# A decode block on one core: the engines' programs written into the main program instead of a block

## The chip, the core and the metric

The kernel runs on one core of a Trainium2 chip. Its time is the device time of one execution in microseconds (us); the median of several runs is given. A profile shows one execution, with times counted from the first instruction of the program to the last (the span). The core has five engines with programs of their own: TensorE (PE; its weight loads are PEld), VectorE (DVE), ScalarE (ACT), GpSimd (POOL) and SyncE (SP), which issues DMAs only. They meet through semaphores.

## The reference

One decode step for a batch of 8: a conditioning vector gives six modulation rows, then a grouped-query attention over a cache of 8192 keys, then a gated feed-forward part. Cut to what is computed:

```python
mod = (silu(c) @ w_mod).reshape(8, 6, 1, 1024)          # sa, ca, ga, sb, cb, gb
h = layernorm(x) * (1 + ca) + sa
q = (h @ wq)                                            # 32 heads of 128, 4 key/value heads
p = softmax(q @ k_cache^T * 128**-0.5)                  # 8 x 32 x 8192
x = x + ga * ((p @ v_cache) @ wo)
h = layernorm(x) * (1 + cb) + sb
g = h @ W_gate; g = g * (g > 0)
x = x + gb * ((g * (h @ W_up)) @ W_down)                # 8 x 1 x 1024, bf16
```

All inputs are bf16. The caches are 67 MB each; with the weights 185.6 MB are read from HBM.

## The kernel before, in words

Everything that is read passes through one ring buffer in SBUF, five slots of 4 MB. SyncE issues all of these loads (line 747), one after the other in an order written out by hand: the query weights, the modulation weights, then 16 pairs of a key block and a value block (two key/value heads of one batch row, 4 MB each), with the output weights between, then the gate, up and down weights. A load that reuses a slot first waits for the last TensorE instruction that read the slot. The small inputs c and x are loaded by ScalarE (line 87).

GpSimd first fills constants. VectorE and ScalarE prepare the conditioning vector; TensorE multiplies it by the modulation weights, then the normalised x by the query weights. The attention is a loop over n, 0 to 17, software-pipelined by hand: in step n TensorE transposes the key block of n (line 426), VectorE and ScalarE copy the transposed keys out of PSUM, TensorE makes the scores (line 422); for n-1 the softmax, the transposition of the weights and the product with the value block follow; for n-2 the sums and the division. Then come the output projection, the second normalisation, gate and up, and the down projection, whose last loads are cut ever smaller (3584 KB to 256 KB). The last two VectorE operations give outR, which goes out in four DMAs, two from SyncE and two from ScalarE (line 87), all counted on one semaphore, osem, 16 each.

The code doesn't call the engines directly. A small graph class collects operations in five lists, one an engine, with what each reads and writes; it thins the dependences out, numbers the semaphores' values, and `emit` writes one list to its engine, operation by operation, with the waits ahead of each (line 117). On TensorE, VectorE and ScalarE the attention's steps 0 to 15 are emitted as a hardware loop of eight turns of two steps (line 158), with waits against a value computed from the turn's number (line 161).

The lists are handed to the engines at the end of the kernel's function. There a block is opened, and each engine's list is emitted in a body of that block; SyncE's body ends with a wait for the four DMAs of the output:

```python
            def body(_, name=name, e=e):
                g.emit(name, e, sems)
                if name == "sp":
                    e.wait_ge(osem, 64)
            starter(body)
```

A body is a stretch of program for one engine. The engine reaches it by a jump from the main program (line 761 is its place in the source) and leaves it by a jump to the block's end. At the block's end, which is written when the context closes (line 269 in the profile), each engine drains, all report to GpSimd by a semaphore event, and GpSimd lets all of them go by another: a closing round. On SyncE the wait for osem is held by the jump that leaves the body. The main program itself begins with four constants on GpSimd and a round of the same kind, the opening round, which is written when the program object is made (line 775).

Of the kernel before, what the change touches and what calls it, by code (L numbers as in the profile page):

```python
# [234 lines left out]
def bass_adaLN_cond__gqa_block_cached__glu_gated_reglu__decode_kernel(  # L235
# [14 lines left out]
    B, _, D = A_x.shape  # L250
    _, G, Sk, Dh = A_k_cache.shape
# [14 lines left out]
    g = _Graph()  # L266
    f32, bf16 = dt.float32, dt.bfloat16

    with ExitStack() as es:
        E = es.enter_context  # L270
# [58 lines left out]
        sems = {e: E(nc.semaphore("m_" + e)) for e in g.prog}  # L329
        csem = E(nc.semaphore("d_c"))  # L330
        xsem = E(nc.semaphore("d_x"))
        osem = E(nc.semaphore("d_o"))
# [412 lines left out]
        for i, (key, at, cols, src, shape, slot) in enumerate(stream):  # L745
# [4 lines left out]
        g.prog["sp"] = head + g.prog["sp"]  # L750
        g.number()

        block_ = E(nc.Block())
        engs = {"sp": (nc.sync, block_.sync), "act": (nc.scalar, block_.scalar), "pool": (nc.gpsimd, block_.gpsimd),
                "dve": (nc.vector, block_.vector), "pe": (nc.tensor, block_.tensor)}
        for name, (e, starter) in engs.items():
            def body(_, name=name, e=e):
                g.emit(name, e, sems)
                if name == "sp":
                    e.wait_ge(osem, 64)  # L760
            starter(body)


# [26 lines left out]
```

## Time and profile before

| what | value |
|---|---|
| median of 3 runs | 438.68 us (438.67 to 438.71) |
| the profiled execution | 438.55 us |
| its span, first to last instruction | 436.6 us |
| mean granted TensorE clock | 0.945 |
| DMA queue of SyncE | 185.61 MB, 98.7% of 16 engines' time |
| busy: PE, ACT, DVE, POOL | 306.9, 208.6, 180.0, 12.7 us |

The execution is 1.95 us longer than the span; what lies in that difference is not in the trace. Rows of the trace name an engine, a line of the source, an operation and the buffers. A q behind an engine's name (SPq) marks work of its sequencer: waiting, jumping, issuing DMAs. It isn't counted as busy. DRAIN is an instruction that lets the engine finish what it has begun, EVENT_SEMAPHORE one that waits for a semaphore or changes it, COMPARE_BRANCH a jump.

### The profile page before, as it was taken

How to read it: one execution, taken by the hardware profiler on the slowest of the kernel's cores; microseconds unless marked ns; L12 is line 12 of the kernel's file. 1: busy time of each engine (PE TensorE's matmuls, PEld its weight loads, DVE VectorE, ACT ScalarE, POOL GpSimd, SP SyncE). 2: the span in 40 equal slices, each digit the busy share in tenths (PEclk: the TensorE clock that was granted, in tenths of full speed). 3: DMA queues.
4: the chain of work that ended last, by engine and by line, in shares of the span. 5: the costliest groups of instructions: out<-in, count | busy, mean ns of one | idle time of the engine just before them, and what ended most of it. 6: DMA issues, size and time to landing. Idle time of an engine off the chain costs nothing.

```text
span 436.6 us, 10734 instructions
## 1 busy us (share of the span) xinstructions
PE 306.9 (70%) x4575; PEld 199.4 (46%) x4575; DVE 180.0 (41%) x384; ACT 208.6 (48%) x246; POOL 12.7 (3%) x52
## 2 busy tenths in 40 slices
PE   0104276889889888787888888778888878755353
PEld 0101024656556555555555556555555555432321
DVE  3600027365463644536264553536354453331111
ACT  2200004676767747675664757576575747400000
POOL 6000000000000000000000000000000000000000
PEclk9999579999999999999999999999999999885778
DMA  8999999999999999999999999999999999999995
GB/s 342 438 446 437 429 431 434 432 428 437 432 441 432 432 432 432 432 435 435 432 432 432 432 432 432 432 432 432 432 432 432 432 432 432 422 435 439 427 422 236
DMA packets 7003, 185.81 MB, mean 426 GB/s; under 512 B 800, under 2 KB 832, under 8 KB 1104
## 3 DMA queue, kind: packets, MB, share of 16 engines
q1 hardware_dynamic: 6928, 185.61, 98.7%
q8 instruction: 9, 0.15, 0.1%
q10 hardware_dynamic: 64, 0.04, 0.0%
q14 instruction: 2, 0.02, 0.0%
HBM read 185.63 MB, written 0.02 MB: 425 GB/s over the span
## 4 chain that ended last, share of the span: by engine, by line
DMA 54%; PE 23%; issue 8%; DVE 8%; ACT 6%; SPq 1%; DVEq 0%; ACTq 0%
DMA ring<-in_A_k_cache_dram 29%; PE PS L426 12%; DMA ring<-in_w_mod_dram 11%; PE PS L422 11%; DMA ring<-in_B_W_down_dram 7%; DMA ring<-in_B_W_up_dram 6%; ACT P L433 3%; DVE KT L430 2%; ACT KT L433 2%; DVE tm L430 1%; DVE ov L430 1%; DVE nm L430 1%; SPq L747 1%; DVE nb L430 0%; DVE rl L430 0%
## 5 line engine op out<-in xcount | busy, mean ns | idle before, releaser
L433 ACT ACTIVATE KT<-PS 128x1024 bf16<-128x1024 bf16 (+1 forms) x130 | 132.1, 1017 | 163.8 <-PE PS L426 137.4
L426 PE MATMUL PS<-identb,ring 128*128 128x128 bf16 x2048 | 152.8, 220 | 19.3 <-DMA ring<-in_A_k_cache_dram 17.6
L430 DVE COPY KT<-PS 128x1024 bf16<-128x1024 bf16 (+1 forms) x129 | 88.9, 689 | 162.5 <-PE PS L426 126.3
L426 PEld LDWEIGHTS PS<-identb,ring 128*128 128x128 bf16 x2048 | 117.0, 98 | 58.5 <-issue 37.3
L422 PE MATMUL PS<-KT,Z 128*32 128x512 bf16 x516 | 51.9, 390 | 0.1
L422 PE MATMUL PS<-ring,pt 128*32 128x256 bf16 x1088 | 49.8, 274 | 0.6 <-DVE pt L430 0.6
L433 ACT ACTIVATE P<-PS,nb 64x1024 bf16<-64x1024 f32 x34 | 37.7, 1109 | 6.2 <-DVE nb L430 4.2
L426 PE MATMUL PS<-identb,P 128*128 128x128 bf16 x272 | 21.0, 221 | 20.2 <-ACT P L433 14.5
L422 PEld LDWEIGHTS PS<-ring,pt 128*32 128x32 bf16 x1088 | 24.5, 95 | 12.8 <-issue 0.8
L422 PE MATMUL PS<-ring,siluT 128*24 128x512 bf16 x96 | 9.8, 584 | 27.5 <-DMA ring<-in_w_mod_dram 27.5
L426 PEld LDWEIGHTS PS<-identb,P 128*128 128x128 bf16 x272 | 15.3, 98 | 26.5 <-DVE KT L430 17.2
L433 ACT ACTIVATE pt<-PS 64x512 bf16<-64x512 bf16 x34 | 20.1, 592 | 13.5 <-PE PS L426 13.2
L430 DVE COPY pt<-PS 64x512 bf16<-64x512 bf16 x34 | 14.4, 422 | 17.7 <-PE PS L426 17.2
L430 DVE TENSOR_REDUCE mp<-PS 128x1 f32<-128x1024 f32 x17 | 20.6, 1214 | 0.0
L422 PEld LDWEIGHTS PS<-KT,Z 128*32 128x32 bf16 x516 | 13.3, 93 | 13.8 <-ACT KT L433 0.5
L422 PE MATMUL PS<-ring,h2T 128*8 128x512 bf16 (+1 forms) x128 | 10.4, 490 | 11.6 <-DMA ring<-in_B_W_up_dram 9.7
L422 PEld LDWEIGHTS PS<-ring,siluT 128*24 128x24 bf16 x96 | 3.1, 125 | 33.5 <-DMA ring<-in_w_mod_dram 28.3
L433 ACT ACT_TABLE_LOAD x11 | 14.1, 1283 | 8.3 <-DMA KT<-in_A_x_dram 8.1
L426 PE MATMUL PS<-identb,KT 128*128 128x128 bf16 (+1 forms) x19 | 1.7, 218 | 18.4 <-DVE KT L430 18.4
L637 POOL CAST ot<-og 128x16 bf16<-128x16 f32 x16 | 4.1, 256 | 288.2 <-DVE og L430 288.2
L422 PE MATMUL PS<-od,selo 128*128 128x128 f32 x36 | 8.8, 326 | 5.1 <-DVE od L430 5.1
L422 PEld LDWEIGHTS PS<-ring,h2T 128*8 128x8 bf16 x128 | 3.5, 108 | 17.8 <-DMA ring<-in_B_W_up_dram 11.0
(99 smaller groups left out, 161.4 us busy)
## 6 DMA issues: line engine op xcount, KB each, us to landing
ring<-in_A_k_cache_dram SPq DMA_DIRECT2D x16, 4096.0 KB, 21.6
ring<-in_A_v_cache_dram SPq DMA_DIRECT2D x16, 4096.0 KB, 30.5
ring<-in_w_mod_dram SPq DMA_DIRECT2D x2, 6144.0 KB, 42.4
ring<-in_A_wq_dram SPq DMA_DIRECT2D x2, 4096.0 KB, 16.8
ring<-in_A_wo_dram SPq DMA_DIRECT2D x2, 4096.0 KB, 28.1
ring<-in_B_W_gate_dram SPq DMA_DIRECT2D x2, 3584.0 KB, 24.8
ring<-in_B_W_up_dram SPq DMA_DIRECT2D x2, 3584.0 KB, 31.0
ring<-in_B_W_down_dram SPq DMA_DIRECT2D x1, 3584.0 KB, 36.1
```

The source lines that it names most:

```text
L422: return pe(lambda e: e.matmul(out_, lhsT, rhs, start=start, stop=stop, skip_group_check=True), reads, writes, block, deps)
L426: return pe(lambda e: e.matmul(out_, in_, ident, start=True, stop=True, is_transpose=True), reads, writes, block)
L430: return g.op("dve", lambda e: getattr(e, name)(*args, **kw), reads, writes)
L433: return g.op("act", lambda e: e.activation(*args, **kw), reads, writes)
L637: pool(lambda e: e.tensor_copy(dst, og[:, n % 2]), reads=[("og", n % 2)], writes=[("ot", n // B)])
L747: o.fn = (lambda e, key=key, src=src, o=o: e.dma_start(place[key], src).then_inc(o.sem, 16))
```

## The change

The block is gone. `emit` is called for the five engines one after the other, in the order SyncE, ScalarE, GpSimd, VectorE, TensorE, and writes their instructions into the main program, behind the opening round. The wait for the output is written last, on SyncE.

```diff
         g.prog["sp"] = head + g.prog["sp"]
         g.number()
 
-        block_ = E(nc.Block())
-        engs = {"sp": (nc.sync, block_.sync), "act": (nc.scalar, block_.scalar), "pool": (nc.gpsimd, block_.gpsimd),
-                "dve": (nc.vector, block_.vector), "pe": (nc.tensor, block_.tensor)}
-        for name, (e, starter) in engs.items():
-            def body(_, name=name, e=e):
-                g.emit(name, e, sems)
-                if name == "sp":
-                    e.wait_ge(osem, 64)
-            starter(body)
+        for name, e in (("sp", nc.sync), ("act", nc.scalar), ("pool", nc.gpsimd), ("dve", nc.vector), ("pe", nc.tensor)):
+            g.emit(name, e, sems)
+        nc.sync.wait_ge(osem, 64)
```

On each engine the operations and their waits stay in the same order. What differs is at the ends: the jump into the body and the jump out of it go, on SyncE the wait that the latter held becomes an instruction of its own, and the block's end goes, that is a drain on each engine, the event by which it reports or is let go, and GpSimd's two events. The opening round stays. The hardware loops stay as they are.

## The prediction

> **What bounds the kernel now.** I read the page first, for the span and the load of each engine.
>
> ```profile
> span 436.6 us, 10734 instructions
> PE 306.9 (70%) x4575; PEld 199.4 (46%) x4575; DVE 180.0 (41%) x384; ACT 208.6 (48%) x246; POOL 12.7 (3%) x52
> DMA  8999999999999999999999999999999999999995
> q1 hardware_dynamic: 6928, 185.61, 98.7%
> q8 instruction: 9, 0.15, 0.1%
> DMA 54%; PE 23%; issue 8%; DVE 8%; ACT 6%; SPq 1%; DVEq 0%; ACTq 0%
> ```
>
> No compute engine is busy for more than 70% of the span, while the one queue that carries the weights and the caches fills 98.7% of sixteen engines' time. The digits of the DMA row are nines from the second slice to the last but one. The kernel is bound by one stream of loads that SyncE issues, and the chain of waits is mostly transfers (54%). So an edit counts only if it moves the start of that stream, stretches it, or lies behind its end. The change touches no operation, load, buffer or semaphore inside the work; it touches the two places where the five programs are joined to the main program. I therefore read the timeline at both ends of the span, then the rows that carry the lines of the frame: L775 (opening round), L761 (jump into the block), L269 (block's end).
>
> The start, from the timeline:
>
> ```profile
> 0.73 0.21 POOL L444 MEMSET identb<- 128x128 bf16 x1 [0.29 <-POOLq L775]
> 0.74 0.89 SPq L747 DMA_DIRECT2D ring<-in_A_wq_dram  x2
> 0.74 0.59 ACTq L87 DMA_DIRECT2D KT<-in_c_dram  x1
> ```
>
> The end, from the timeline of the last 4 us, and SyncE's own waits there:
>
> ```profile
> 432.99 0.09 PEld L422 LDWEIGHTS PS<-ring,hmT 128*8 128x8 bf16 x4 [0.52 <-DMA ring<-in_B_W_down_dram]
> 433.00 0.39 PE L422 MATMUL PS<-ring,hmT 128*8 128x256 bf16 x4 [0.23 <-DMA ring<-in_B_W_down_dram]
> 433.89 0.42 DVE L430 TENSOR_TENSOR outR<-ov,x1R 128x256 bf16<-128x256 f32 x1
> 434.34 0.71 SPq L87 DMA_DIRECT2D out_dram<-outR  x2
> SPq L269 <- DMA out_dram<-outR: 1.1, 1, 1.1
> SPq L269 <- PEq L269: 0.2, 1, 0.2
> ```
>
> The last weights land, four matmuls and two vector operations follow, the output goes out from 434.34 for 0.71 us (to 435.05), SyncE then waits 1.1 us for the output to land (436.2), and only after that does the closing round run, with a second wait of 0.2 us in SyncE. The instructions of that round carry the line of the context that closes, L269:
>
> ```profile
> L269 POOLq EVENT_SEMAPHORE  x2: 17/17/17, 436.4 to 436.5; - x2
> L269 POOLq DRAIN  x1: 341/341/341, 384.5 to 384.5; - x1
> L269 PEldq DRAIN  x1: 442/442/442, 433.0 to 433.0; - x1
> L269 DVEq DRAIN  x1: 464/464/464, 433.9 to 433.9; - x1
> L269 ACTq DRAIN  x1: 239/239/239, 435.0 to 435.0; - x1
> L269 SPq COMPARE_BRANCH  x1: 33/33/33, 436.2 to 436.2; - x1
> L269 SPq DRAIN  x1: 7/7/7, 436.4 to 436.4; - x1
> L269 SPq EVENT_SEMAPHORE  x1: 17/17/17, 436.5 to 436.5; - x1
> L269 PEldq EVENT_SEMAPHORE  x1: 51/51/51, 436.5 to 436.5; - x1
> ```
>
> The columns of a row are the shortest, median and longest duration in ns, then the first and the last start in us. The reader is to see who is early and who is late. GpSimd reaches the end at 384.5, TensorE at 433.0, VectorE at 433.9, ScalarE at 435.0; each drains there beside the others' work. SyncE comes last: its jump out of the block is held by the wait for the output, leaves at 436.2, and everything after it (drain, gather on GpSimd, release to all) stands in the open.
>
> **The change part by part.**
>
> *The jump into the block, one an engine.* The query for L761 answers
>
> ```profile
> nothing on L761; most used: ['L426', 'L422', 'L161', 'L430', 'L433', 'L158', 'L747', 'L637', 'L775', 'L556', 'L444', 'L269', 'L117', 'L87', 'L446']
> L775 SPq EVENT_SEMAPHORE  x1: 17/17/17, 0.7 to 0.7; - x1
> L747 SPq DMA_DIRECT2D ring<-in_A_wq_dram x2: 410/414/418, 0.7 to 1.2; - x2
> ```
>
> so no such jump was executed, or none was recorded. SyncE is let go by the opening round at 0.7 and issues its first load at 0.74. Two consecutive loads take 0.89 us together, of which 410 and 418 ns are their own, so 0.06 us lies between two issues with no jump at all. That is as long as the whole gap after the opening round can well be (0.74 less 0.7 and 0.017). The jump is worth at most that gap, 0.06 us; I take nothing, since the gap without a jump is as long. The opening round itself stays, and with it every start in the timeline.
>
> *The closing round.* Removed are five drains and six semaphore events (two on GpSimd, one on each of the four others). The drains of PE, DVE, ACT and POOL (442, 464, 239 and 341 ns) save nothing: the wait for the output covers them, since the latest, ACT's from 435.0, is over at 435.3, 0.9 us before SyncE. If that cover were gone the longest would cost 0.46 us; it isn't touched. On the path stands only what follows SyncE's wake-up at 436.2. The span ends at 436.6 with PE's event (436.5 and 51 ns), so the round costs 0.4 us. One instruction must stay to hold the wait for the output: it becomes a plain semaphore event, 17 to 33 ns by the rows of SyncE's event and jump. 0.40 − 0.03 = 0.37 us. The starts are printed to a tenth, so the bounds are 0.27 and 0.47.
>
> *The wait for the output* (four arrivals of 16) is kept on SyncE. Nothing is queued behind it, and nobody else waits for it, so its 1.1 us stays as it is. The order of loads on SyncE's queue and of everything on the other engines is the same, so the stream of loads has nothing to react to.
>
> *What lies outside the span.* The profiled execution took 438.55 us for a span of 436.6: 1.95 us lie around it, of which the trace tells nothing. They hold whatever stands behind the programs. Before the change all five engines get there together at 436.6; after it GpSimd gets there at 384.5 and SyncE at 436.2. A price for that has to be bounded: nothing below, and above what a slower engine's steps exceed SyncE's by. PE's event takes 51 ns where SyncE's takes 17, so if all the 1.95 us were such steps on PE, SyncE alone would need a third, 0.65, and up to 1.3 us would go. I take zero, because SyncE is still last and must take the same steps as ever; 1.3 stays for the range. The Trainium skill ("Runtime: NRT & Kernel Launch", "The ~15µs preamble/postamble breakdown") says that behind the kernel come a barrier that waits for all engines (about 1.5 us), a reset of semaphores (1.5) and a second barrier (2). By that rule the resets start only when SyncE has arrived, early engines gain nothing, and the time is that of my sum. Its 5 us are more than the 1.95 us here, so this case's time can't hold them all, and no row shows which part it holds.
>
> *Sum.* The profiled execution becomes 438.55 − 0.37 = 438.18. The median of the three runs shown, 438.68, lies 0.13 above the profiled one; the same step off it gives 438.31, so I predict **438.3 us**. This is a gain of 0.08%, less than the 0.2% (0.88 us) that a measurement of this kernel can tell from no change.
>
> **The rivals.**
>
> *The end behind the programs shrinks too (faster).* Engines that arrive early take their steps there under cover of the output's landing. For it: four engines are done 0.9 us or more before SyncE, and PE's event takes three times SyncE's. Against it: SyncE's own steps are not covered by anything. Time: down to 438.31 − 1.3 = 437.0 at most; over 0.2% faster from a saving of 0.51 us outside the span on. Chance 0.25.
>
> *Nothing is gained.* What stands behind the programs joins the engines again, and a SyncE that comes late to that join costs as much as the removed round, 0.37 us. For it: the trace ends there. Against it: SyncE was last in the old round as well, and after that round a further join would have been paid already. 438.7 us. Chance 0.10.
>
> *TensorE has to fetch its last instructions late (slower).* The page counts 9 packets of instructions, 0.15 MB, and the window just before the last weights land holds one of them:
>
> ```profile
> q8 instruction: 1, 0.02, 6.0%
> PEld PS L422 <- issue: 20.9, 60, 2.0
> ```
>
> (the first row is the DMA view of 432 to 433 us, the second is from the table of waits). A fetch thus falls just ahead of the last four matmuls at 433.00. If the shorter programs moved the edge of a fetched piece into these four, PE would stand still in the open: the longest wait of a weight load in which nothing but its own sequencer is seen is 2.0 us, so 438.31 + 2.0 = 440.3. It decides as soon as the stall is over 1.25 us (0.88 + 0.37). Against it: in PE's program the drain and the event that go stand behind those matmuls, and nothing ahead of them is in the trace that could go, so the edge should stay where it is. Chance 0.05. The Trainium skill ("Runtime: NRT & Kernel Launch", "Instruction fetch mechanics") says that fetches come in pieces of 16 KiB ahead of straight-line code and that a taken branch out of the window stalls. The piece size agrees (0.15 MB in 9 packets). By that rule a jump less can only help here, and the time would be the forecast's.
>
> **How the numbers follow.** The forecast has 0.60, the faster rival 0.25, no gain 0.10, the late fetch 0.05. The forecast and no gain both lie within 0.2% of 438.68 (437.80 to 439.56): 0.70. Faster by over 0.2%: 0.25. Slower: 0.05. The range reaches up to 438.9, which takes in no gain and the runs' and builds' own spread (half of the 0.37 again above 438.68), and leaves out the late fetch. Downward it goes to 437.2, most of the way to the faster rival's end at 437.0, of which I leave out the last fifth.
>
> **What would show it right or wrong.** Right: the span is 436.2, its last instruction is SyncE's wait for the output at 436.2; no drain is left at the ends of the other four programs; first issues still at 0.73 and 0.74; the output's DMAs at 434.3; execution less span still 1.95. The faster rival is right if execution less span falls below 1.4; no gain if it rises to 2.3. The late fetch shows as an idle PE between the last landing and the last four matmuls, with the output's DMAs later than 434.3. The prediction is wrong in its ground if the first load moves from 0.74, or if the stream's end at 433.0 moves by more than a tenth: then the frame would touch the loads, which I hold it doesn't.

## The result, and the profile after

The changed kernel takes 438.05 us (median of 22 runs, 437.85 to 438.34), the kernel before 438.64 (22 runs, 438.45 to 439.15): 0.59 us less, a ratio of means of 0.9986 with a 95% interval of 0.9979 to 0.9992. Run once more in another group of runs (e11 below) it took 438.06 against 438.73, a ratio of means of 0.998 with an interval of 0.997 to 0.999. By the medians it is faster by 0.13 and 0.15%, inside the 0.2% band that held most of the chance, and 0.25 us below the predicted 438.3. The prediction took 0.2% as the least that can be told from no change; with this many runs the interval ends below 1, so less than that can be told.

The profiled execution took 438.01 us, for this span and these loads (the page of the changed kernel):

```profile
span 436.3 us, 10723 instructions
PE 307.2 (70%) x4575; PEld 200.1 (46%) x4575; DVE 180.0 (41%) x384; ACT 208.4 (48%) x246; POOL 12.6 (3%) x52
q1 hardware_dynamic: 6928, 185.61, 98.8%
q8 instruction: 9, 0.15, 0.1%
```

The work is the same to the instruction: equal counts on all five engines, equal bytes, equal fetches. Eleven instructions are gone. The start, from the timeline:

```profile
0.73 0.20 POOL L444 MEMSET identb<- 128x128 bf16 x1 [0.29 <-POOLq L769]
0.74 0.88 SPq L747 DMA_DIRECT2D ring<-in_A_wq_dram  x2
```

The opening round (now line 769) ends as before, and the first load starts at 0.74 as before, so the missing jump into the block gave nothing. The end, from the timeline:

```profile
433.05 0.09 PEld L422 LDWEIGHTS PS<-ring,hmT 128*8 128x8 bf16 x4 [0.17 <-DMA ring<-in_B_W_down_dram]
433.96 0.42 DVE L430 TENSOR_TENSOR outR<-ov,x1R 128x256 bf16<-128x256 f32 x1
434.41 0.71 SPq L87 DMA_DIRECT2D out_dram<-outR  x2
```

then SyncE's own waits (us in total, times, longest):

```profile
SPq L755 <- DMA out_dram<-outR: 1.1, 1, 1.1
```

and the row of line 755, the wait for the output (shortest, median and longest duration in ns, then the first and the last start in us):

```profile
L755 SPq EVENT_SEMAPHORE  x1: 17/17/17, 436.3 to 436.3; - x1
```

In this execution the last four weight loads start 0.06 us later than in the one before (433.05 against 432.99), within the wobble of the stream from run to run; the output leaves at 434.41, SyncE waits the same 1.1 us, and its 17 ns event is the last instruction of the program. Nothing follows it. From SyncE's wake-up to the end of the span there were 0.4 us, and there are 17 ns. The traces hold starts to the nanosecond, finer than the rows print them: before, the jump starts at 436.210 and the span ends at 436.581, 371 ns later, so 0.35 us went.

What the page doesn't show is the rest. Execution less span was 438.55 − 436.6 = 1.95 before; it is 438.01 − 436.3 = 1.71 after. In the changed kernel this difference is steadier than the time, since the wobble of the stream drops out of it: it lies between 1.64 and 1.80 in its 22 runs, the time between 437.85 and 438.34. Its median is 1.96 before (the 35 runs beside e1 to e4) and 1.68 after (22 runs). So the gain has two parts: 0.30 within the span (438.63 − 1.96 = 436.67 to 438.05 − 1.68 = 436.37) and 0.28 outside it. On one chip, in e11's group, the parts are 0.42 and 0.25.

Two limits go with this measure. The trace doesn't say whether the part outside lies ahead of the program or behind it; as all edits stand at the programs' ends, I take it to lie behind, which is not shown. And in 12 of the 97 runs of the kernel before that lie beside the experiments it was 2.28 to 2.55, while none of the 150 runs of kernels without the block (the table below) exceeded 2.25. The medians hardly feel these runs; why they occur is open.

### The profile page after: what moved, and what is told of

Same layout as the page of the kernel before. It is cut to its first block, busy times and chain, and to the rows that moved or that the text cites. A ratio compares the mean times of both kernels' runs of the same rounds, so it can differ in the third digit from the quotient of the medians.

```text
span 436.3 us, 10723 instructions
## 1 busy us (share of the span) xinstructions
PE 307.2 (70%) x4575; PEld 200.1 (46%) x4575; DVE 180.0 (41%) x384; ACT 208.4 (48%) x246; POOL 12.6 (3%) x52
## 4 chain that ended last, share of the span: by engine, by line
DMA 54%; PE 23%; DVE 9%; issue 8%; ACT 5%; SPq 0%; DVEq 0%; ACTq 0%; POOL 0%
DMA ring<-in_A_k_cache_dram 34%; PE PS L422 13%; DMA ring<-in_w_mod_dram 11%; PE PS L426 11%; DMA ring<-in_B_W_down_dram 8%; ACT P L433 3%; DVE KT L430 2%; ACT KT L433 2%; DVE tm L430 2%; DVE ov L430 1%; DVE nm L430 1%; DVE mp L430 1%; DVE rl L430 0%; DVE nb L430 0%; DVE qT L430 0%
## 5 line engine op out<-in xcount | busy, mean ns | idle before, releaser
L422 PE MATMUL PS<-ring,siluT 128*24 128x512 bf16 x96 | 8.6, 531 | 27.6 <-DMA ring<-in_w_mod_dram 27.6
```

Of the source, the lines that this page charges most:

```text
L422: return pe(lambda e: e.matmul(out_, lhsT, rhs, start=start, stop=stop, skip_group_check=True), reads, writes, block, deps)
```

## The experiments

All start from the changed kernel. In the table each time is a median, "outside" is the median of execution less span, and the span is the time less that. The kernel before ran beside each group; its outside median was 1.96, 1.96 and 1.94 in the groups of e1 to e4, e5 to e8 and e9 to e11, which ran on three chips. Each run's span is on record to a tenth, so differences of a few hundredths between rows mean little.

| run | what is last | runs | us | before, same group | outside | span |
|---|---|---|---|---|---|---|
| before | round, then all five | 35 | 438.63 | | 1.96 | 436.67 |
| changed | SyncE | 22 | 438.05 | 438.64 | 1.68 | 436.37 |
| e11 | SyncE, once more | 12 | 438.06 | 438.73 | 1.69 | 436.37 |
| e10 | SyncE; drains on four | 12 | 438.05 | 438.73 | 1.61 | 436.44 |
| e6 | VectorE | 11 | 438.23 | 438.75 | 1.82 | 436.41 |
| e5 | ScalarE | 11 | 438.19 | 438.75 | 1.86 | 436.33 |
| e3 | TensorE | 12 | 438.40 | 438.63 | 1.96 | 436.44 |
| e8 | four, not GpSimd | 11 | 438.43 | 438.75 | 1.97 | 436.46 |
| e7 | GpSimd | 11 | 438.47 | 438.75 | 2.16 | 436.31 |
| e2 | all five, no round | 12 | 438.56 | 438.63 | 2.13 | 436.43 |
| e9 | round of events, no drains | 12 | 438.41 | 438.73 | 1.84 | 436.57 |
| e1 | round, no block | 12 | 438.61 | 438.63 | 1.97 | 436.64 |
| e4 | two rounds, no block | 12 | 438.98 | 438.63 | 2.06 | 436.92 |

**e1: the closing round put back, without the block.**

```diff
         nc.sync.wait_ge(osem, 64)
+        nc.all_engine_barrier()
```

> The changed kernel with one closing round (drains, gather on GpSimd, release) put back behind the wait for the output; no block, no jumps. Measured so far: 438.64 before, 438.05 after, a difference of 0.59; in the profiles 0.3 of it within the span, and execution less span 1.95 before, 1.71 after. Theory A (a slow engine let go late: with a round all five leave together at the very end, and the slowest walks what stands behind the programs in the open): the round alone brings everything back, 438.6, execution less span 1.95, span longer by 0.3 than in the changed kernel. Theory J (the jumps and the block's layout cost the part outside the span): the span grows by 0.3 but execution less span stays at 1.7, 438.35.

Measured: 438.61 us, ratio to before 0.9996 (0.9982 to 1.001), 1.97 outside. Theory A's numbers came, theory J's did not: the round alone brings back both parts, and the block's jumps and layout cost nothing that the medians can tell. The rows of the round in its trace, with the wait for the output (L755) first:

```profile
L755 SPq EVENT_SEMAPHORE  x1: 17/17/17, 436.5 to 436.5; - x1
L756 SPq DRAIN  x1: 7/7/7, 436.5 to 436.5; - x1
L756 POOLq EVENT_SEMAPHORE  x2: 17/17/17, 436.6 to 436.6; - x2
L756 PEldq EVENT_SEMAPHORE  x1: 51/51/51, 436.7 to 436.7; - x1
```

SyncE's drain follows its wait within the printed tenth (436.5 and 436.5), where in the kernel before it followed the jump from 436.2 to 436.4. To the nanosecond, the drain starts 61 ns after SyncE's wake-up in e1 and 156 ns after it in the kernel before, and from the wake-up to the end of the span it is 276 and 371 ns. So in these two traces the jump out of the block costs about 0.1 us, and the round 0.26 beside the 17 ns of the wait; the two median times, 0.02 apart, don't resolve the 0.1.

**e2: all five engines wait for the output, no round.**

```diff
-        nc.sync.wait_ge(osem, 64)
+        for e in (nc.sync, nc.scalar, nc.gpsimd, nc.vector, nc.tensor):
+            e.wait_ge(osem, 64)
```

> The changed kernel, but each of the five engines ends with a wait for the output, so all leave together at the output's landing without any drain, gather or release. Theory A: leaving together is what costs outside the span, so execution less span returns to 1.9 to 1.95 while the span stays at 436.3: 438.25 to 438.3. Theory R (the round itself leaves something behind, such as its drains or semaphores, that costs later): execution less span stays at 1.7 and the time at 438.05.

Measured: 438.56 us, 2.13 outside, span 436.43. The span is that of the changed kernel, and there is neither drain nor gather nor release; yet the time is that of before, nearly. Theory R falls: it isn't something that a round leaves behind. Theory A's sign is right and its size too small by 0.2. All five end together in the trace:

```profile
L756 SPq EVENT_SEMAPHORE  x1: 17/17/17, 436.4 to 436.4; - x1
L756 ACTq EVENT_SEMAPHORE  x1: 17/17/17, 436.4 to 436.4; - x1
L756 POOLq EVENT_SEMAPHORE  x1: 17/17/17, 436.4 to 436.4; - x1
L756 PEldq EVENT_SEMAPHORE  x1: 51/51/51, 436.4 to 436.4; - x1
L756 DVEq EVENT_SEMAPHORE  x1: 21/21/21, 436.4 to 436.4; - x1
```

**e3: TensorE alone leaves last.**

```diff
-        nc.sync.wait_ge(osem, 64)
+        nc.tensor.wait_ge(osem, 64)
```

> The changed kernel with the wait for the output on TensorE instead of SyncE: TensorE alone leaves last. Theory A with TensorE as the slow engine (its event takes 51 ns against 17): execution less span 1.95 or a little more, 438.3. If all engines' ways out are equally long, or the number of engines that leave together counts: 1.7 and 438.05. If TensorE joins later steps in a better place than SyncE does, less than 1.7.

Measured: 438.40 us, 1.96 outside. One instruction moved from SyncE to TensorE costs 0.28 us outside the span and nothing clear inside (436.44 against 436.37). This is as much as the change gained there. The execution profiled took 439.67 us, as its last loads landed over 1 us later than in the others; execution less span is 439.67 − 437.7 = 1.97 in it all the same. Its last row:

```profile
L755 PEldq EVENT_SEMAPHORE  x1: 51/51/51, 437.7 to 437.7; - x1
```

**e4: two rounds.**

```diff
         nc.sync.wait_ge(osem, 64)
+        nc.all_engine_barrier()
+        nc.all_engine_barrier()
```

> The changed kernel with two closing rounds behind the wait for the output. The price of a round within the span: by the sum of the prediction 0.37 for the first; a second with nothing to wait for costs 0.3 to 0.4 more. Theory A: execution less span is that of one round (1.95), since the engines leave together once; the time is that of one round plus 0.3 to 0.4, about 439.0. If a round itself costs outside the span too (theory R), execution less span rises by 0.25 again, to 2.2, and the time to 439.2.

Measured: 438.98 us, span 436.92, 2.06 outside. The second round adds 0.28 to the span and 0.09 outside. The first is the price of a round, as expected (0.3 to 0.4, a little under). The outside part is nearer to theory A's zero than to theory R's 0.25, but it is not zero. The trace shows the second round, with nothing for the engines to finish since the first:

```profile
L757 SPq DRAIN  x1: 7/7/7, 436.7 to 436.7; - x1
L757 POOLq DRAIN  x1: 41/41/41, 436.7 to 436.7; - x1
L757 POOLq EVENT_SEMAPHORE  x2: 17/17/17, 436.8 to 436.9; - x2
```

Its drains take 7 ns on SyncE and 41 on GpSimd (8, 13 and 19 on ScalarE, TensorE and VectorE); most of the rest of the 0.3 us is the way of one event to GpSimd and of one back.

**e5, e6, e7: ScalarE, VectorE, GpSimd alone leave last.** The edit is that of e3 with `nc.scalar`, `nc.vector` and `nc.gpsimd`:

```diff
-        nc.sync.wait_ge(osem, 64)
+        nc.scalar.wait_ge(osem, 64)      # e5; nc.vector in e6, nc.gpsimd in e7
```

> The changed kernel with the wait for the output on ScalarE alone. Execution less span so far (medians): 1.96 before, 1.68 with the wait on SyncE, 1.96 on TensorE, 1.97 with one round, 2.13 with a wait on all five. Theory A, read as one way out per engine, each of a length of its own: ScalarE's event takes 17 ns like SyncE's, so 1.7 and 438.05. If only SyncE's place behind the programs is a good one: 1.95, 438.3.

> The changed kernel with the wait for the output on VectorE alone. Theory A: its event takes 21 ns, between SyncE's 17 and TensorE's 51, so 1.7 to 1.75 and 438.1. If only SyncE's place is a good one: 1.95, 438.3.

> The changed kernel with the wait for the output on GpSimd alone. With five waits execution less span was 2.13, more than with a round (1.97), and in the round GpSimd is let go 0.1 us before TensorE. Theory A with GpSimd as the longest way out: 2.15, 438.5. If GpSimd's way is as short as SyncE's by its event of 17 ns: 1.7, 438.05, and the 2.13 must come from the number of engines that leave together.

Measured: 1.86, 1.82 and 2.16 outside, with spans from 436.31 to 436.41. GpSimd is the longest, as expected of theory A. But the length doesn't follow how long the engine's event takes, which was my expectation for the other two:

```profile
L755 ACTq EVENT_SEMAPHORE  x1: 17/17/17, 436.4 to 436.4; - x1
```

```profile
L755 POOLq EVENT_SEMAPHORE  x1: 17/17/17, 436.1 to 436.1; - x1
```

(ScalarE's last row in e5, GpSimd's in e7.) Both take 17 ns, as SyncE's does, and are followed by 1.86 and 2.16 us where SyncE's is followed by 1.68. That half of the theory is wrong. The other reading, 1.95 on every engine but SyncE, doesn't fit either: 1.86 and 1.82 lie between, and 2.16 above.

**e8: four engines wait, GpSimd doesn't.**

```diff
-        nc.sync.wait_ge(osem, 64)
+        for e in (nc.sync, nc.scalar, nc.vector, nc.tensor):
+            e.wait_ge(osem, 64)
```

> The changed kernel with a wait for the output on SyncE, ScalarE, VectorE and TensorE, not on GpSimd. If GpSimd's way out made the 2.13 of five waits: 1.96 as with TensorE alone, 438.4. If the number of engines that leave together counts: about 2.1, 438.5.

Measured: 1.97 outside, TensorE's number, and 438.43 us. It isn't the count of engines. Together e2, e3, e7 and e8, the programs without a round, follow one rule: the part outside the span is that of the slowest engine among those that leave last. With all five it is GpSimd's (2.16 from GpSimd's own end, which is 0.04 ahead of the end of TensorE's 51 ns event, so 2.12 against 2.13), with four it is TensorE's (1.97 against 1.96). The rule doesn't carry over to the programs with a round. There GpSimd's last event ends 0.09 ahead of TensorE's (87 ns in the traces of before, e1 and e9, 88 in e4), so it would give 2.07. Two rounds measured 2.06, but one round 1.97 (e1) and 1.96 (before).

**e9: a round without drains.**

```diff
         nc.sync.wait_ge(osem, 64)
+        nc.all_engine_barrier(sem_only=True)
```

> The changed kernel with a closing round of events alone, without drains, behind the wait for the output. The prediction holds that the drains of the four early engines cost nothing: then the span is that of one full round less SyncE's own drain (7 ns and the gap ahead of it, some 0.05), so 436.55 against 436.61 with a full round, execution less span 1.96, and 438.5 in all. If the drains carry a part of the price, the time lies clearly below that, at 438.2 to 438.3.

Measured: 438.41 us, span 436.57, 1.84 outside. The span came as expected: without any drain the round still costs 0.20, against 0.27 with them (medians from two chips). In the traces it takes 187 ns from GpSimd's first event to the end of the span, and 183 in e1, so the drains of the early engines are no part of its price. Outside I expected 1.96 and got 0.12 less; by the rule of e8, with GpSimd's 2.07, it is 0.23 less. The engine that ends last is TensorE again:

```profile
L756 PEldq EVENT_SEMAPHORE  x2: 51/51/51, 433.1 to 436.4; - x2
L756 SPq EVENT_SEMAPHORE  x2: 17/565/1113, 435.2 to 436.4; - x2
```

SyncE's first event has here taken over the wait for the output (1113 ns). Why 1.84 follows is open.

**e10: drains without a round.**

```diff
         nc.sync.wait_ge(osem, 64)
+        for e in (nc.scalar, nc.gpsimd, nc.vector, nc.tensor):
+            e.drain()
```

> The changed kernel with a drain at the end of ScalarE's, GpSimd's, VectorE's and TensorE's program and no events. If the drains lie under the output's landing, as predicted: span 436.37 and execution less span 1.68, 438.05, the changed kernel's own numbers. If a drain delays the way out of its engine beyond SyncE's: more than 1.75 outside the span.

Measured: 438.05 us, the changed kernel's time. The drains are as long as in the kernel before or longer, and cost nothing, since SyncE is last by far:

```profile
L757 PEldq DRAIN  x1: 600/600/600, 433.2 to 433.2; - x1
L757 ACTq DRAIN  x1: 250/250/250, 435.4 to 435.4; - x1
L755 SPq EVENT_SEMAPHORE  x1: 17/17/17, 436.6 to 436.6; - x1
```

Outside it reads 1.61, 0.08 less than e11 with the same engine last. So programs that end on SyncE alone differ by 0.08. Among those that end with a round the spread is larger, 1.84 to 2.06 (e9, before, e1, e4), and the rule above doesn't explain it.

**e11: the changed kernel once more.** No edit; it runs on the chip of e9 and e10.

> The changed kernel once more, on the same chip as the two others. SyncE alone leaves last: span 436.37, execution less span 1.68, 438.05, which is 0.59 less than the kernel before. If the small difference between the two kernels was one of the chip or of the day, it moves by more than 0.2.

Measured: 438.06 us, 1.69 outside, 0.67 below before. The gain came again, on one chip with e9 and e10.

## Why the prediction was right, and where it was off

The ground held: the frame doesn't touch the loads. The first load is at 0.74 in both traces, the stream's end moved by 0.06 us, less than the tenth that I had set, and with the drains of four engines back in place the time stays (e10). That the stream's end kept within the tenth is luck: across the profiles of the experiments, which differ only behind it, the same weight loads start between 433.00 (e7) and 433.29 (e6), and at 434.44 in e3. A single profile can't give that sign.

The jump into the block, taken at nothing, is nothing: no start moved, and e1, without the block but with the round, repeats the time of before.

The closing round, taken at 0.37 with bounds 0.27 and 0.47, measured 0.30 within the span from the medians of the two kernels (0.42 in e11's group, 436.79 to 436.37) and 0.35 from their two traces. The term was sized well. It held two things that the prediction didn't part: the round (0.27 when it is put back in e1, 0.28 for a second one in e4) and the jump out of the block, about 0.1 us by the traces of before and e1.

The cover of the drains was right: 250 to 600 ns of drains in e10 cost nothing, as the latest of them is over 0.9 us before SyncE's wait.

The term that was mis-sized is "what lies outside the span". I took zero, "because SyncE is still last and must take the same steps as ever", and kept up to 1.3 us for the range. It measured 0.28 (1.96 to 1.68), and the sign that I had named for the forecast, execution less span still 1.95, read 1.71. So the forecast was right on the span, and the faster rival was at work beside it at a fifth of its largest price. That the result lies in the range is owed to this rival, for which the range reached down to 437.2; the sum had missed the term. What the runs show is that it matters who is late: with a round at the end (e1) or TensorE late alone (e3) the 1.96 comes back, and of the five engines SyncE has the least behind it. That the slow ones among the five set the 1.96 of the kernel before is argued from this; the rule of e8 taken by itself would give 2.07 there. The rival's reason, that engines which arrive early have their part covered, fits these runs but isn't seen in any. Its measure was wrong: I scaled by the length of TensorE's event against SyncE's (51 to 17 ns), and ScalarE and GpSimd with 17 ns are slower than SyncE too. It did not reach the 0.51 us from which the time would have been over 0.2% faster, and the sign that I named for it, a difference below 1.4, did not come.

The rule of the Trainium skill that I set beside this term ("Runtime: NRT & Kernel Launch", "The ~15µs preamble/postamble breakdown": a barrier that waits for all engines, then resets) would have given the sum alone. The runs differ from what I drew from it, that early engines gain nothing: 0.28 us depend on who is late. A barrier that passes through the engines in a fixed order could do that as well as steps of different lengths on each engine. No run here tells these apart, as the trace ends with the program; which of them it is stays open.

No gain (a late SyncE pays the round again outside) is refuted by the 1.68. The late fetch did not come: the count of fetches is the same (9 packets), and the last four weight loads of TensorE start after an idle time of 0.17 us that ended with the landing (the row of 433.05).

## What to carry to other kernels

Where one engine waits for the last output, a closing round of all engines behind that wait buys nothing here and costs about 0.3 us in the open, and here as much again outside the span; drains on engines that are done earlier cost nothing. Put the last wait on one engine only and choose it: SyncE was the cheapest, and GpSimd dearer than it by almost 0.5 us. For effects this small outside the program compare the medians of execution less span beside those of the time, since the wobble of the work drops out and a tenth of a microsecond becomes visible.

## What the runs showed that I had not expected

The time outside the span depends on which engine ends last: 1.68 us for SyncE, 1.82 VectorE, 1.86 ScalarE, 1.96 TensorE, 2.16 GpSimd (11 to 22 runs each), with a spread of up to 0.08 us between programs without a round that end alike. The order of SyncE, TensorE and GpSimd is beyond that spread; that of VectorE and ScalarE is not. Behind a round the spread is 0.22 us, so there the order says little. The drain of an engine with nothing to finish takes 7 to 41 ns (e4), so a second round, 0.28 us, is nearly all signalling.
